# Local attention, gated layer and soft mixture of experts on one core: q and k of the last two batches read in 32-column pieces and turned by VectorE

## The chip, the cores and the metric

One Trainium2 chip, one of its cores. The metric is the device time of one execution in microseconds: 482.99 us as the median of three runs before the change (480.85 to 483.46). Times inside the execution come from one profiled execution and count from the start of its span. TensorE does the matrix products, VectorE and ScalarE elementwise work, GpSimd (POOL in the rows) elementwise work on SBUF alone, and SyncE (SP) issues the transfers between HBM and SBUF.

## The reference

```python
scores = (1 / sqrt(D)) * q @ k.T              # 4 batches, 8 heads, 576 positions, 64 columns
mask: heads 0-3 keep the last 32 positions;
      heads 4-7 keep every 4th of the last 128
attn = exp(scores - max) / (sum + 1e-9); x = attn @ v      # x: 2304 tokens x 512
h = x @ w_in; g = h - tanh(h); x = g @ w_out               # 512 -> 2048 -> 512
logits = x @ phi                                           # 32 slots
d = softmax(logits over tokens); c = softmax(logits over slots)
slot_in = d.T @ x; per expert: slot_out = relu(slot_in @ w1) @ w2
out = c @ slot_out
```

## The kernel before

Batches and chunks are numbered from 0, as in the code; the change is on batches 2 and 3, the third and the fourth.

The work is written out by hand in one order for all engines. The attention of batch 0 comes first. Then come four chunks of 512 tokens for the gated layer (the 64 tokens that each batch has left over follow later as a fifth, shorter part), and each of the first three chunks carries the attention of the next batch beside it: chunk 0 that of batch 1 (`mixed_step`, with the conversion of the weights), chunk 1 that of batch 2 and chunk 2 that of batch 3 (`phase_step`). Chunk 3 carries none. A chunk has 8 steps of two tiles of 128 hidden columns. A tile of `emit_h` is 12 products of 512 columns on TensorE (L505 to L507), followed by tanh on ScalarE (L511) and a subtraction on VectorE (L514). Its result g goes to the logits (`emit_logits`, L520, on TensorE) and is turned in 32x32 blocks on VectorE (`emit_gT`, L527).

A `phase_step` issues, in this order: the first tile; the denominators of the scores of the step before (`emit_norm`: VectorE L329 and L331, GpSimd L332); tanh and subtraction; in steps 0 and 2 a piece of the softmax over the chunk before (`sm_one`); tile turns; the second tile with its tanh and subtraction; the logits of the tiles of the step before; transposes of the probabilities (`emit_trans`, L341, copied out by ScalarE); q and k of one pair (`emit_qk`, L270); two units of scores (`emit_scores`, L308); two units of values (`emit_pv`, L362); loads; and in steps 0 to 2 another softmax piece. The pieces are `sm_a` (takes the logits out of PSUM and forms their maximum, at the chunk's end), `sm_b` and `sm_c` (the maximum over tokens, exponentials), `sm_d` (transposes, with the copy L609), `sm_e` (the sums for the slots, L643 on TensorE, L650 on VectorE) and `sm_c2` (the softmax over slots, L620 to L628).

Heads go in pairs, four pairs a batch, in the order of `PO = (2, 3, 0, 1)`: the dilated heads first. A pair has three units of scores, a batch twelve, two in each of steps 0 to 5. `load_qk` reads q and k of a pair with 96 rows on the partitions, and `emit_qk` brings the 64 columns onto the partitions: six transposes each for k and q on TensorE into PSUM, from where VectorE (k) and ScalarE (q, scaled by 1/8) copy them into a ring of two places (`qks`). For the dilated heads the copy also sorts the positions, so that those of one class lie next to each other. Scores of batches 2 and 3 are masked by an addition on VectorE (L314) and reduced to their maximum (L317); ScalarE does the exponentials (L320).

Before the change `an.qk` does pair 0 at the end of the chunk before and pairs 1 to 3 in steps 0, 2 and 3:

```python
            if an:
                an.trans(s)
                if s in (0, 2, 3):
                    an.qk(max(1, s))
                an.score(2 * s)
```

Raw q and k, v, weights, x and expert weights live in 16 equal places of SBUF (`unit`); a transfer that gets a place waits until its last reader is done. All transfers stand in SP's queue in program order. Late in the kernel the weights of the experts arrive in places that the layer's weights and tiles have left.

Of the kernel before, what the change touches and what calls it, by code (L numbers as in the profile page):

```python
# [8 lines left out]
F32 = mybir.dt.float32  # L9
# [5 lines left out]
ALU = mybir.AluOpType  # L15
# [16 lines left out]
MASKPE = 2  # L32
PO = (2, 3, 0, 1)
RAW = {
    ("out", 0): 0, ("out", 2): 1, ("out", 4): 2, ("in", 0): 3, ("in", 2): 0, ("in", 4): 1, ("out", 6): 2, ("in", 6): 3,
# [27 lines left out]
def moe_kernel(ctx: ExitStack, tc: tile.TileContext, q, k, v, w_in, w_out, phi, w1, w2, out):  # L63
    nc = tc.nc
# [4 lines left out]
    NP = H // 2  # L69
# [139 lines left out]
    def load_qk(b, p):  # L209
# [13 lines left out]
        raws[b, p] = t  # L223

    def load_v(b, p, eng):

# [59 lines left out]
    def emit_scores(b, i):  # L286
# [11 lines left out]
        for c in range(nb):  # L298
            for x in range(2):
                if nb == 4:  # L300

                    r2, qi = divmod(2 * u + c // 2, 3)
                    q0 = 288 * (c % 2) + 144 * r2
                    q0, k0 = q0 + nq * qi, q0 + max(0, nq * qi - 32)
                else:
                    q0, k0 = nq * (nb * u + c), max(0, nq * (nb * u + c) - 32)
                r = slice(64 * x, 64 * x + 64)
                nc.tensor.matmul(  # L308
                    ps[64 * x:64 * x + nr, c, :], lhsT=qT[b, p][r, q0:q0 + nr], rhs=kT[b, p][r, k0:k0 + nk],
                    start=not by_pe, stop=True, skip_group_check=True,  # L310
                )
# [213 lines left out]
    def emit_gT(ch, ft, g):  # L525

        nc.vector.transpose(out=gt[:, ft, :], in_=g)  # L527
# [230 lines left out]
    class Attn:  # L758
# [5 lines left out]
        def load(self, nqk, nv):  # L764
            while self.nqk < min(nqk, NP) or self.nv < min(nv, NP):
                if self.nqk < min(nqk, NP):
                    load_qk(self.b, PO[self.nqk])
                    self.nqk += 1
                if self.nv < min(nv, NP):
                    load_v(self.b, PO[self.nv], nc.sync)  # L770
                    self.nv += 1

        def turn(self, s):
# [5 lines left out]
            if 0 < s <= NU // 2:  # L779
                for i in (2 * s - 2, 2 * s - 1):  # L780
                    emit_trans(self.b, i)

        def qk(self, p):
            for n in range(2):
                emit_qk(self.b, PO[p], n)

# [36 lines left out]
    with tc.manual_schedule():  # L823
# [59 lines left out]

        def mixed_step(an, ch, s, xh, xl, gs):

# [48 lines left out]

        def phase_step(an, ch, s, xh, xl, gs):

# [5 lines left out]
            emit_sub(pa, gs[a])  # L942
            if s in (0, 2):
                sm_one()
# [8 lines left out]
            if an:  # L953
                an.trans(s)
                if s in (0, 2, 3):
                    an.qk(max(1, s))
                an.score(2 * s)
                an.score(2 * s + 1)
                an.values(s)
                an.load(*{0: (3, 2), 2: (4, 3), 3: (4, 4)}.get(s, (0, 0)))  # L960
            if s < 3:
                sm_one()

        an = Attn(1)
        an.nqk, an.nv = 2, 1
        for ch in range(4):
# [13 lines left out]
            for s in range(NFT // 2):  # L980
                (phase_step if ch else mixed_step)(an, ch, s, xh, xl, gs)
                if ch < 2 and s > 4:
                    if s == 5:
                        nxt = Attn(ch + 2)
                    nxt.load(*((2, 0) if s == 5 else (2, 1)))
                room[0] += sum(ROOM.get((ch, f), 0) for f in (2 * s, 2 * s + 1))
                load_experts()
            if ch:
                emit_logits(ch, NFT - 2, gs[NFT - 2])
            if nxt:  # L990
                nxt.qk(0)
            emit_logits(ch, NFT - 1, gs[NFT - 1])
            sm_queue(ch, 4)
            emit_gT(ch, NFT - 2, gs[NFT - 2])
            emit_gT(ch, NFT - 1, gs[NFT - 1])
            an = nxt
        prev = None
# [173 lines left out]
```

## Time and profile before

| | |
|---|---|
| median of three runs | 482.99 us (480.85 to 483.46) |
| the profiled execution | 480.95 us, its span 479.2 us |
| TensorE products / VectorE / ScalarE / GpSimd busy | 442.2 / 258.1 / 207.5 / 63.6 us |
| chunk 1 (157.68 to 236.97) | 79.29 us |
| chunk 2 (236.97 to 316.30) | 79.33 us |
| transposes of q and k (L270), whole kernel | 192 |

The span is the time from the first to the last instruction; the rest of the execution's time lies around it. Busy time of TensorE overlaps from one product to the next, so the length of a group is read from its start to the start of what follows.

### The profile page before, as it was taken

What the parts mean: (1) busy time and instruction counts of PE and PEld (TensorE: products, weight loads), DVE (VectorE), ACT (ScalarE), POOL (GpSimd) and SP (SyncE); (2) the same over time, 40 slices, a digit from 0 to 9 for tenths busy, and PEclk for the clock granted to TensorE, in tenths of its full rate; (3) what the DMA queues carried; (4) which work ended last, traced back from release to release, by engine and by line L of the source; (5) the groups of instructions that cost most, each with busy time, mean ns of one, the idle gap of its engine ahead of it and who ended that gap; (6) DMA issues with size and microseconds to landing.
All of it is one profiled execution on the core that took longest, in us unless ns stands there. A gap on an engine that the chain in (4) does not pass through costs nothing.

```text
span 479.2 us, 11573 instructions
## 1 busy us (share of the span) xinstructions
PE 442.2 (92%) x4711; PEld 325.9 (68%) x4711; DVE 258.1 (54%) x631; ACT 207.5 (43%) x699; POOL 63.6 (13%) x87
## 2 busy tenths in 40 slices
PE   6989888997999999999999999999999999999971
PEld 4766556776767877787786777777777879645320
DVE  1455589877976646656544775552843351232031
ACT  4877366555542373654354555422111222213131
POOL 3311313332332020111011021100000000010000
PEclk9999998998999999999999999999999999999996
DMA  9999954968252301411410310229000789999938
GB/s 247 223 248 305 255 189 133 269 219 224 91 177 60 75 0 24 102 53 51 105 29 3 87 39 1 90 77 363 1 1 0 253 320 408 348 406 409 406 152 331
DMA packets 60740, 81.15 MB, mean 169 GB/s; under 512 B 35600, under 2 KB 39440, under 8 KB 60688
## 3 DMA queue, kind: packets, MB, share of 16 engines
q1 hardware_dynamic: 60688, 80.42, 52.9%
q8 instruction: 37, 0.61, 0.6%
q14 instruction: 15, 0.12, 0.1%
HBM read 71.50 MB, written 8.91 MB: 168 GB/s over the span
## 4 chain that ended last, share of the span: by engine, by line
PE 62%; DVE 15%; ACT 9%; DMA 7%; issue 2%; POOL 2%; SPq 0%; DVEq 0%; ACTq 0%; POOLq 0%
PE h L505 12%; PE h L507 11%; PE h L506 11%; ACT mem L320 5%; DMA ex<-in_moe_w_dram 4%; PE lg L520 4%; PE mm L643 4%; PE mm L308 4%; PE h L727 3%; PE mm L362 2%; DVE cva L446 2%; PE mm L341 2%; DMA raww<-in_moe_w_out_dram 2%; PE mm L270 2%; DVE gt L527 2%
## 5 line engine op out<-in xcount | busy, mean ns | idle before, releaser
L505 PE MATMUL h<-xhi,whi 128*128 128x512 f32 x256 | 105.9, 414 | 1.1 <-DVE whi L101 0.7
L507 PE MATMUL h<-xhi,wlo 128*128 128x512 f32 x256 | 100.9, 394 | 2.0 <-POOL wlo L460 2.0
L506 PE MATMUL h<-xlo,whi 128*128 128x512 f32 x256 | 100.8, 394 | 0.0
L511 ACT ACTIVATE mem<-h 128x512 f32<-128x512 f32 x60 | 35.7, 596 | 100.3 <-PE h L507 100.1
L514 DVE TENSOR_TENSOR mem<-h,mem 128x512 f32<-128x512 f32 x60 | 41.1, 684 | 57.2 <-ACT mem L511 57.1
L505 PEld LDWEIGHTS h<-xhi,whi 128*128 128x128 f32 x256 | 48.6, 190 | 17.4 <-issue 5.3
L507 PEld LDWEIGHTS h<-xhi,wlo 128*128 128x128 f32 x256 | 48.5, 189 | 14.4 <-POOL wlo L460 3.7
L506 PEld LDWEIGHTS h<-xlo,whi 128*128 128x128 f32 x256 | 48.6, 190 | 8.9 <-DVE xlo L394 0.2
L332 POOL TENSOR_TENSOR mem<-mem 128x320 f32<-128x320 f32 (+1 forms) x48 | 33.0, 703 | 130.6 <-DVE mem L329 81.2
L394 DVE TENSOR_TENSOR xlo<-mm,xhi 128x144 fp32r<-128x144 f32 (+4 forms) x72 | 16.7, 269 | 37.0 <-ACT xhi L101 36.3
L320 ACT ACTIVATE mem<-mem 128x80 f32<-128x80 f32 (+1 forms) x84 | 29.7, 355 | 14.4 <-DVE mem L317 14.4
L308 PE MATMUL mm<-qk 64*64 64x96 f32 (+2 forms) x672 | 33.6, 243 | 2.3 <-ACT qk L278 2.1
L320 ACT ACTIVATE mem<-mm,mem 128x80 f32<-128x80 f32 (+1 forms) x84 | 26.8, 335 | 16.3 <-DVE mem L317 16.2
L527 DVE STREAM_TRANSPOSE gt<-mem 128x512 f32<-128x512 f32 x52 | 33.4, 684 | 0.0
L101 ACT COPY mem<-mm 96x384 f32<-96x384 f32 (+4 forms) x64 | 26.3, 436 | 15.8 <-PE mm L341 8.5
L308 PEld LDWEIGHTS mm<-qk 64*64 64x64 f32 (+1 forms) x672 | 26.9, 131 | 8.4 <-ACT qk L278 3.8
L341 PE MATMUL mm<-mem 112*80 112x112 f32 (+1 forms) x168 | 24.0, 272 | 6.8 <-ACT cvb L437 2.7
L460 POOL TENSOR_TENSOR wlo<-cvb,whi 128x512 fp32r<-128x512 f32 x16 | 20.6, 1287 | 73.4 <-DVE whi L101 33.7
L362 PE MATMUL mm<-mem,v 80*64 80x48 f32 (+1 forms) x672 | 26.0, 226 | 0.5 <-ACT mem L101 0.5
L362 PEld LDWEIGHTS mm<-mem,v 80*64 80x64 f32 (+1 forms) x672 | 22.1, 137 | 5.4 <-issue 2.2
L270 PE MATMUL mm<-mem,rqk 96*128 96x96 f32 x192 | 21.3, 257 | 4.2 <-DMA rqk<-in_k_dram 4.1
L341 PEld LDWEIGHTS mm<-mem 112*80 112x80 f32 (+1 forms) x168 | 16.1, 122 | 12.1 <-POOL mem L332 7.1
(169 smaller groups left out, 673.8 us busy)
## 6 DMA issues: line engine op xcount, KB each, us to landing
ex<-in_moe_w_dram SPq DMA_DIRECT2D x20, 1024.0 KB, 9.3
gt<-in_moe_w_dram SPq DMA_DIRECT2D x8, 1024.0 KB, 13.5
gt<-in_moe_w_out_dram SPq DMA_DIRECT2D x7, 1024.0 KB, 7.9
gt<-in_moe_w_in_dram SPq DMA_DIRECT2D x7, 1024.0 KB, 7.0
wo_dram<-cva SPq DMA_DIRECT2D x16, 256.0 KB, 6.5
mem<-in_moe_w_dram SPq DMA_DIRECT2D x4, 1024.0 KB, 9.9
wo<-wo_dram SPq DMA_DIRECT2D x4, 1024.0 KB, 6.8
out_dram<-o SPq DMA_DIRECT2D x8, 512.0 KB, 4.8
```

Source lines behind the costliest of these rows:

```text
L270: nc.tensor.transpose(ps[:, r, :], raw[:, 3 * th + r if p < NP // 2 else 2 * r + th], ident[0:96, 0:96])
L308: nc.tensor.matmul(ps[64 * x:64 * x + nr, c, :], lhsT=qT[b, p][r, q0:q0 + nr], rhs=kT[b, p][r, k0:k0 + nk], start=not by_pe, stop=True, sk ...
L320: nc.scalar.activation(out=pr[:, c, :], in_=ps[:, c, :], func=ACTF.Exp, bias=nm[:, c:c + 1], accum_out=sm[:, c:c + 1],)
L332: nc.gpsimd.tensor_tensor(out=pr, in0=pr, in1=rc.unsqueeze(2).to_broadcast([128, nb, nk]), op=ALU.mult)
L341: nc.tensor.transpose(ps[:, c, :], pr[0:P, c, :], ident[0:P, 0:P])
L362: nc.tensor.matmul(o[64 * hh:64 * hh + 64, col:col + nq], lhsT=vt[b, p](n, hh), rhs=pt[:, c, 64 * x:64 * x + nq], start=True, stop=True,)
L505: nc.tensor.matmul(ps, lhsT=wh, rhs=xh[:, kt, :], start=(n == 0), stop=False)
L506: nc.tensor.matmul(ps, lhsT=wh, rhs=xl[:, kt, :], start=False, stop=False)
L507: nc.tensor.matmul(ps, lhsT=wl, rhs=xh[:, kt, :], start=False, stop=(n == KT - 1))
L511: nc.scalar.activation(out=g, in_=ps, func=ACTF.Tanh)
L514: nc.vector.tensor_tensor(out=g, in0=ps, in1=g, op=ALU.subtract)
L527: nc.vector.transpose(out=gt[:, ft, :], in_=g)
```

## The change

Batches 2 and 3 (`VB`) read q and k in eight transfers a pair. The partition is a position within a block of 32 (and the half of the columns, and the head or, for the dilated heads, the parity of the position), and the pieces that follow each other on it are 32 columns, 128 bytes, of one position each. GpSimd scales the raw q by 1/8 in place, and two instructions on VectorE turn k and q in 32x32 blocks straight into the ring's place. For the dilated heads the positions of one class are then every second column, and the score products step by two on both sides. `turn_qk` comes right after the subtraction of the first tile, in steps 0, 1, 3 and 4 for pairs 0 to 3. The last logits of a chunk, `sm_a` and the last two tile turns (`last_posts`) are issued in step 0 of the next chunk behind its first tile's subtraction; the softmax pieces then come one place later.

```diff
--- before.py
+++ after.py
@@ -31,6 +31,7 @@
 CAL = 2.29
 MASKPE = 2
 PO = (2, 3, 0, 1)
+VB = (2, 3)
 RAW = {
     ("out", 0): 0, ("out", 2): 1, ("out", 4): 2, ("in", 0): 3, ("in", 2): 0, ("in", 4): 1, ("out", 6): 2, ("in", 6): 3,
     ("out", 8): 2, ("out", 10): 1, ("in", 8): 2, ("in", 10): 3, ("out", 14): 2, ("in", 14): 3,
@@ -222,6 +223,39 @@
                 nc.sync.dma_start(out=t[:, n], in_=src.rearrange("h (x a) d -> (h x) (a d)", a=12))
         raws[b, p] = t
 
+    def load_qk_blocks(b, p):
+
+        t = unit("rqk", [128, 2, S])
+        for n, src in enumerate((q, k)):
+            src = src[b, 2 * p:2 * p + 2]
+            for x in range(2):
+                if p < NP // 2:
+                    rows = src[x].rearrange("(t l) d -> l t d", l=32)
+                else:
+                    rows = src.rearrange("h (m l i) d -> i l h m d", l=32, i=2)[x]
+                for dh in range(2):
+                    dst = t[64 * x + 32 * dh:64 * x + 32 * dh + 32, n]
+                    cols = slice(32 * dh, 32 * dh + 32)
+                    if p < NP // 2:
+                        nc.sync.dma_start(out=dst.rearrange("p (t d) -> p t d", d=32), in_=rows[:, :, cols])
+                    else:
+                        nc.sync.dma_start(
+                            out=dst.rearrange("p (h m d) -> p h m d", h=2, d=32), in_=rows[:, :, :, cols]
+                        )
+        raws[b, p] = t
+
+    def turn_qk(b, p):
+
+        if not qks:
+            t = sb.tile([128, 2, 2 * S], F32, tag="qk", name="qk")
+            qks.append(Ring([t[:, 0], t[:, 1]]))
+        t = raws[b, p]
+        nc.gpsimd.tensor_scalar(out=t[:, 0], in0=t[:, 0], scalar1=0.125, scalar2=None, op0=ALU.mult)
+        qT[b, p] = qks[0].next()
+        kT[b, p] = qT[b, p][:, S:2 * S]
+        nc.vector.transpose(out=kT[b, p], in_=t[:, 1])
+        nc.vector.transpose(out=qT[b, p][:, 0:S], in_=t[:, 0])
+
     def load_v(b, p, eng):
 
         t = unit("v", [96, 24 * D])
@@ -297,16 +331,21 @@
             )
         for c in range(nb):
             for x in range(2):
+                step = 1
                 if nb == 4:
 
                     r2, qi = divmod(2 * u + c // 2, 3)
                     q0 = 288 * (c % 2) + 144 * r2
                     q0, k0 = q0 + nq * qi, q0 + max(0, nq * qi - 32)
+                    if b in VB:
+                        q0, k0 = (288 * (c % 2) + r2 + 2 * (t - 288 * (c % 2) - 144 * r2) for t in (q0, k0))
+                        step = 2
                 else:
                     q0, k0 = nq * (nb * u + c), max(0, nq * (nb * u + c) - 32)
                 r = slice(64 * x, 64 * x + 64)
                 nc.tensor.matmul(
-                    ps[64 * x:64 * x + nr, c, :], lhsT=qT[b, p][r, q0:q0 + nr], rhs=kT[b, p][r, k0:k0 + nk],
+                    ps[64 * x:64 * x + nr, c, :], lhsT=qT[b, p][r, q0:q0 + step * (nr - 1) + 1:step],
+                    rhs=kT[b, p][r, k0:k0 + step * (nk - 1) + 1:step],
                     start=not by_pe, stop=True, skip_group_check=True,
                 )
         pr = prs.next()[:, 0:nb * nk].rearrange("p (c k) -> p c k", c=nb)
@@ -764,7 +803,7 @@
         def load(self, nqk, nv):
             while self.nqk < min(nqk, NP) or self.nv < min(nv, NP):
                 if self.nqk < min(nqk, NP):
-                    load_qk(self.b, PO[self.nqk])
+                    (load_qk_blocks if self.b in VB else load_qk)(self.b, PO[self.nqk])
                     self.nqk += 1
                 if self.nv < min(nv, NP):
                     load_v(self.b, PO[self.nv], nc.sync)
@@ -779,10 +818,6 @@
             if 0 < s <= NU // 2:
                 for i in (2 * s - 2, 2 * s - 1):
                     emit_trans(self.b, i)
-
-        def qk(self, p):
-            for n in range(2):
-                emit_qk(self.b, PO[p], n)
 
         def trans(self, s):
             if 0 < s <= NU // 2:
@@ -881,7 +916,7 @@
             nc.vector.tensor_tensor(out=part[:, :, 1, :], in0=c, in1=part[:, :, 0, :].bitcast(F32), op=ALU.subtract)
             cst[b] = part
 
-        def mixed_step(an, ch, s, xh, xl, gs):
+        def mixed_step(an, ch, s, xh, xl, gs, posts):
 
             a, b = 2 * s, 2 * s + 1
             if s == 0:
@@ -932,7 +967,7 @@
                 emit_logits(ch, a - 1, gs[a - 1])
             emit_logits(ch, a, gs[a])
 
-        def phase_step(an, ch, s, xh, xl, gs):
+        def phase_step(an, ch, s, xh, xl, gs, posts):
 
             a, b = 2 * s, 2 * s + 1
             pa, gs[a] = emit_h(xh, xl, a), gring.next()
@@ -940,7 +975,11 @@
                 an.norms(s - 1)
             emit_tanh(pa, gs[a])
             emit_sub(pa, gs[a])
-            if s in (0, 2):
+            if an and s in QKS:
+                turn_qk(an.b, PO[QKS.index(s)])
+            if s == 0:
+                posts()
+            elif s < 3:
                 sm_one()
             for n in range(0 if s == 2 else max(0, a - 2), 0 if s == 1 else a):
                 emit_gT(ch, n, gs[n])
@@ -952,8 +991,6 @@
                 emit_logits(ch, a - 1, gs[a - 1])
             if an:
                 an.trans(s)
-                if s in (0, 2, 3):
-                    an.qk(max(1, s))
                 an.score(2 * s)
                 an.score(2 * s + 1)
                 an.values(s)
@@ -961,8 +998,9 @@
             if s < 3:
                 sm_one()
 
+        QKS = (0, 1, 3, 4)
         an = Attn(1)
-        an.nqk, an.nv = 2, 1
+        an.nqk, an.nv, posts = 2, 1, None
         for ch in range(4):
             xh, xl = xhi[ch], xlo[ch]
             if ch == 3:
@@ -978,7 +1016,7 @@
                 gring = gts
             gs, nxt = {}, None
             for s in range(NFT // 2):
-                (phase_step if ch else mixed_step)(an, ch, s, xh, xl, gs)
+                (phase_step if ch else mixed_step)(an, ch, s, xh, xl, gs, posts)
                 if ch < 2 and s > 4:
                     if s == 5:
                         nxt = Attn(ch + 2)
@@ -987,13 +1025,16 @@
                 load_experts()
             if ch:
                 emit_logits(ch, NFT - 2, gs[NFT - 2])
-            if nxt:
-                nxt.qk(0)
-            emit_logits(ch, NFT - 1, gs[NFT - 1])
-            sm_queue(ch, 4)
-            emit_gT(ch, NFT - 2, gs[NFT - 2])
-            emit_gT(ch, NFT - 1, gs[NFT - 1])
-            an = nxt
+
+            def last_posts(ch=ch, gs=gs):
+                emit_logits(ch, NFT - 1, gs[NFT - 1])
+                sm_queue(ch, 4)
+                emit_gT(ch, NFT - 2, gs[NFT - 2])
+                emit_gT(ch, NFT - 1, gs[NFT - 1])
+
+            if ch == 3:
+                last_posts()
+            an, posts = nxt, last_posts
         prev = None
         for s in range(NFT // 2):
             a = 2 * s
```

VectorE where chunk 1 begins; before, with the two copies of k (`COPY qk`) of pair 0 and of pair 1:

```order
L514 TENSOR_TENSOR mem<-h,mem 128x512
L101 COPY qk<-mm 128x3x2x48 x2
L552 COPY mem<-lg 128x128
L554 TENSOR_REDUCE mem<-mem 128x1
L527 STREAM_TRANSPOSE gt<-mem 128x512 x2
L514 TENSOR_TENSOR mem<-h,mem 128x512
L562 TENSOR_REDUCE mem<-mm 1x32
```

and VectorE at the same place now, where the first row holds the last subtraction of chunk 0 and the first of chunk 1:

```order
L553 TENSOR_TENSOR mem<-h,mem 128x512 x2
L256 STREAM_TRANSPOSE qk<-rqk 128x576
L257 STREAM_TRANSPOSE qk<-rqk 128x576
L591 COPY mem<-lg 128x128
L593 TENSOR_REDUCE mem<-mem 128x1
L566 STREAM_TRANSPOSE gt<-mem 128x512 x2
L553 TENSOR_TENSOR mem<-h,mem 128x512
L353 TENSOR_TENSOR mem<-mm,mem 128x320
```

The turns of pair 0 stand between the first tile's subtraction and `sm_a`; the masks (L353, before L314) follow the second tile's subtraction with no copies between.

VectorE in step 3 of chunk 1, from the denominators on; before:

```order
L329 TENSOR_SCALAR mem<-mem 128x4
L331 RECIPROCAL mem<-mem 128x4
L514 TENSOR_TENSOR mem<-h,mem 128x512
L527 STREAM_TRANSPOSE gt<-mem 128x512 x2
L514 TENSOR_TENSOR mem<-h,mem 128x512
L101 COPY qk<-mm 128x3x96 x2
L314 TENSOR_TENSOR mem<-mm,mem 128x288
```

and VectorE in step 3 now:

```order
L368 TENSOR_SCALAR mem<-mem 128x4
L370 RECIPROCAL mem<-mem 128x4
L553 TENSOR_TENSOR mem<-h,mem 128x512
L256 STREAM_TRANSPOSE qk<-rqk 128x576
L257 STREAM_TRANSPOSE qk<-rqk 128x576
L566 STREAM_TRANSPOSE gt<-mem 128x512 x2
L553 TENSOR_TENSOR mem<-h,mem 128x512
L353 TENSOR_TENSOR mem<-mm,mem 128x288
```

The two turns have moved ahead of the tile turns and of the second subtraction, where the two copies stood behind them.

GpSimd in chunk 1 now, where before the row of the scaling (L253) was not there:

```order
L253 TENSOR_SCALAR rqk<-rqk 128x576
L371 TENSOR_TENSOR mem<-mem 128x320 x2
L253 TENSOR_SCALAR rqk<-rqk 128x576
L633 COPY mem<-mem 128x512
L371 TENSOR_TENSOR mem<-mem 128x320 x4
L253 TENSOR_SCALAR rqk<-rqk 128x576
L371 TENSOR_TENSOR mem<-mem 128x288 x2
```

Each scaling but the first stands behind the two multiplies of its step.

## Rows read from the trace of the kernel before

**Rows 1.** Windows of chunks 1 and 2: length, busy us and instructions by engine, clock, DMA.
```profile
157.68:236.97 79.29, 78.21 (x892) 61.34 (x889) 46.19 (x120) 40.63 (x152) 8.68 (x13) 1.00 0.21 49
236.97:316.30 79.33, 77.23 (x880) 60.29 (x876) 46.36 (x120) 40.22 (x150) 8.68 (x13) 1.00 0.19 45
```

**Rows 2.** TensorE in order of time where chunk 2 begins, and where chunk 3 begins.
```profile
235.47 1.21 PE L270 MATMUL mm<-mem,rqk 96*128 96x96 f32 x12
236.62 0.43 PE L520 MATMUL lg<-mem 128*32 128x128 f32 x8
236.97 0.50 PE L505 MATMUL h<-xhi,whi 128*128 128x512 f32 x1
...
239.86 0.48 PE L505 MATMUL h<-xhi,whi 128*128 128x512 f32 x1
...
315.94 0.43 PE L520 MATMUL lg<-mem 128*32 128x128 f32 x8 [0.62 <-DVE mem L514]
```

**Rows 3.** TensorE in order of time, end of step 0 of chunk 1.
```profile
163.40 1.16 PE L270 MATMUL mm<-mem,rqk 96*128 96x96 f32 x12
164.48 1.32 PE L308 MATMUL mm<-qk 64*64 64x80 f32 x32
165.74 0.24 PE L569 MATMUL mm<-mem 1*32 1x1 f32 x8
```

**Rows 4.** Groups by line and shape, whole kernel: count, busy us, mean ns, idle before.
```profile
L514 DVE TENSOR_TENSOR mem<-h,mem 128x512 f32<-128x512 f32 x60 | 41.1, 684 | 57.2 <-ACT mem L511 57.1
L511 ACT ACTIVATE mem<-h 128x512 f32<-128x512 f32 x60 | 35.7, 596 | 100.3 <-PE h L507 100.1
L527 DVE STREAM_TRANSPOSE gt<-mem 128x512 f32<-128x512 f32 x52 | 33.4, 684 | 0.0
L460 POOL TENSOR_TENSOR wlo<-cvb,whi 128x512 fp32r<-128x512 f32 x16 | 20.6, 1287 | 73.4 <-DVE whi L101 33.7 <-DVE mem L329 30.2 <-issue 4.8
L332 POOL TENSOR_TENSOR mem<-mem 128x320 f32<-128x320 f32 x24 | 16.9, 720 | 67.5 <-DVE mem L329 48.6 <-DVE mem L331 10.1 <-ACT cva L437 6.5
L101 DVE COPY qk<-mm 128x288 f32<-128x288 f32 x20 | 10.9, 599 | 0.4 <-PE mm L270 0.4
```

**Rows 5.** VectorE, ScalarE and TensorE in order of time, steps 0 to 2 of chunk 1.
```profile
165.66 0.47 DVE L314 TENSOR_TENSOR mem<-mm,mem 128x320 f32<-128x320 f32 x1
...
178.16 0.58 ACT L609 COPY mem<-mm 128x512 f32<-128x512 f32 x1
...
178.83 4.47 PE L643 MATMUL mm<-gt,mem 32*32 32x512 f32 x128
```

**Rows 6.** TensorE in step 2 of chunk 1, VectorE in step 2 of chunk 2.
```profile
187.54 1.35 PE L270 MATMUL mm<-mem,rqk 96*128 96x96 f32 x12
...
268.29 1.18 DVE L101 COPY qk<-mm 128x288 f32<-128x288 f32 x2
```

**Rows 7.** GpSimd and TensorE in order of time, step 3 of chunk 1.
```profile
197.47 1.40 POOL L332 TENSOR_TENSOR mem<-mem 128x320 f32<-128x320 f32 x2 [16.91 <-DVE mem L329]
...
198.24 1.26 PE L341 MATMUL mm<-mem 112*80 112x112 f32 x8 [0.74 <-POOL mem L332]
199.34 1.16 PE L270 MATMUL mm<-mem,rqk 96*128 96x96 f32 x12
200.43 1.31 PE L308 MATMUL mm<-qk 64*64 64x96 f32 x24
```

**Rows 8.** Groups by line and shape: weight loads of transposes, without and with a step of two.
```profile
L538 PEld LDWEIGHTS mm<-mem 128*128 128x128 f32 x32 | 3.4, 140 | 1.6 <-issue 1.2 <-DVE tb L650 0.2 <-ACT g L540 0.2
...
L742 PEld LDWEIGHTS mm<-mem 128*128 128x128 f32 x16 | 2.5, 205 | 2.9 <-issue 2.9
```

**Rows 9.** SP's issue of k, all landings of L217, and the window of these loads.
```profile
188.93 1.25 SPq L217 DMA_DIRECT2D rqk<-in_k_dram  x2
...
DMA to landing us min/median/max: 2.7/4.8/9.1
...
188.90:199.00 10.10, 9.26 (x109) 7.33 (x110) 6.22 (x21) 5.84 (x26) 1.40 (x2) 1.00 0.50 105
```

## The prediction

> **What bounds the kernel now.** I read the busy time by stage first, then TensorE's order of time through chunks 1 and 2, then what VectorE, ScalarE and GpSimd do beside it. The windows of the two chunks [rows 1] are what the change works on: TensorE is busy 78.21 of 79.29 us in chunk 1 and 77.23 of 79.33 in chunk 2 at full granted clock, VectorE 46 and ScalarE 40 of the same time. So an instruction taken off TensorE is worth its length there, as long as nothing else becomes late. What follows (chunk 3, the remainder, the experts) starts from TensorE's progress: expert places and the weight slots become free as TensorE finishes with them, so I let a gain made before 316 us pass through to the end in full.
>
> The order of time at a chunk's end [rows 2] shows the transposes standing as a filler: twelve of them between the logits of tile 14 and those of tile 15, from 235.47 to 236.62. At the end of chunk 2, where there is no next batch, the same place shows 0.62 us of waiting for VectorE's subtraction. In step 0 [rows 3] they take 163.40 to 164.48. Nothing waits for q and k data in these chunks.
>
> **The change part by part.**
>
> 1. *Chunk ends, before chunks 1 and 2.* Twelve transposes go. The logits of tile 15 move behind the next chunk's first tile, so the subtraction they need is long done there and no new gap opens. 236.62 less 235.47 is 1.15 us each [rows 2], two chunks: -2.3.
>
> 2. *Step 0.* 164.48 less 163.40 is 1.08 each, two chunks: -2.2. The cover: scores 0 and 1 now need VectorE's two turns. After the first tile VectorE waits for tanh (0.60 by the row), subtracts (0.68), and turns k and q. A turn of 128x512 takes 0.684, so 576 columns are estimated at 0.684 x 576/512 = 0.77; the four in a row are 0.60+0.68+1.54 = 2.8 us [rows 4], and with hand-overs some 2.9. TensorE meanwhile does the moved logits (0.35, 236.97 less 236.62) and the second tile (a tile takes 2.89, 236.97 to 239.86), 3.2 us [rows 2]. It fits with 0.3 us to spare. GpSimd's scaling is done early here, since the data landed a chunk step before.
>
> 3. *Step 1* gives something back. VectorE's turns of pair 1 stand ahead of the softmax piece that moved here from step 0 (the running maximum and, on ScalarE, its exponential), and ScalarE's tanh of the second tile and its copies of the transposed probabilities stand behind that. GpSimd must multiply two units (0.72 each) before it scales q; the scaling of 576 columns lies between 0.72 (the multiply of 320) and 1.287 x 576/512 = 1.45 (the two-input subtraction of 512) [rows 4]; I take 1.0, as it has one input. Following this chain: the masks of step 0 start at about 164.1 instead of 165.66, so everything on ScalarE and VectorE behind them can be 1.5 early, while TensorE is 2.2 early; the copy that the slot sums of step 2 wait for, which ended at 178.74 just ahead of them at 178.83 [rows 5], comes some 1.3 early. Of 2.2 gained at that point 1.3 is left: +0.9 in chunk 1, and +1.1 in chunk 2, where the moved piece has one more exponential. Both: +2.0 (between +1.0 and +3.0).
>
> 4. *Step 2.* The transposes that start at 187.54 go (1.35 with the last one's tail), -1.3. In chunk 2 VectorE is the late one (four rescalings and four turns ahead); there its two copies (1.18) go, and I count -1.2 [rows 6]. Together -2.5.
>
> 5. *Step 3.* TensorE waits for GpSimd before the probabilities already (0.74), because VectorE came late to the denominators [rows 7]. Now VectorE has subtraction, k turn, the wait for GpSimd's scaling (which starts when the multiplies end, 198.87), and q turn ahead of score 6: 198.87 + 1.0 + 0.77 = 200.6, on the old clock. TensorE, without its transposes from 199.34, would be ready at 199.4. So the 1.09 that goes is replaced by a wait of 1.2: +0.1 each, and +0.1 to +0.3 in chunk 2: +0.4 together (-0.5 to +1.2 with the two ends of GpSimd's price). What is late next is VectorE's subtraction of the second tile, behind two turns and two tile turns; it has until the second tile of step 4.
>
> 6. *Step 4.* The turn is needed for score 9 alone, behind two tiles, logits, probabilities and score 8; 0. ScalarE loses two copies of q a pair; it hid them. VectorE's balance is two turns (1.54) for two copies (2 x 0.599): +0.3 a pair on an engine that is busy under 60%.
>
> 7. *End of chunk 2.* The wait of 0.62 for the subtraction goes [rows 2]: -0.6.
>
> 8. *Scores of the dilated heads* now read every second column for both operands: six steps with 32 passes each (two units, four blocks, two halves, two passes a float32 product), in pairs that run side by side, so 96 pairs of passes. Now 32 passes take 165.74 less 164.48, 1.26 us: 79 ns a pair [rows 3]. The only row with such a step is the weight load of the experts' transposes: 205 ns where the same shape without a step takes 140 [rows 8], 65 more for 128 columns, or 33 for 64. Low end 0, if weight loads stay hidden behind the other half's pass and moving columns cost nothing; a quarter of 33 ns exposed gives 96 x 8 = +0.8; high end 79 more a pair, both sides at half pace, 96 x 79 = +7.6. I take +0.8, because the loads overlap the passes of the other half. [...]
>
> 9. *Loads.* Eight transfers of 72 KB instead of two or four; SP issues one in 0.63 (1.25 for two), so 5.0 us a pair instead of 2.5, landing 4.8 after issue [rows 9]. In 188.90 to 199.00 the queue moved pair 3's q and k and 8 blocks of v, 2304 + 1728 pieces of 256 bytes, at 0.50 of 16 engines: 81 us for 4032, 20 ns each. 4608 pieces at that price are 5.8 us a pair over 16 engines. Pair 3 is the tight one: loaded at the end of step 2 and now turned in step 4, over 13 us later; 5.0 + 4.8 fits. Price 0. SP moves nothing else past them that is urgent.
>
> Sum: -2.3 - 2.2 + 2.0 - 2.5 + 0.4 - 0.6 + 0.8 = -4.4. The profiled execution took 480.95, so 476.6; the median of the runs is 482.99, 2.0 above it, which gives 478.6. I forecast 478.0, nearer to the median.
>
> **Rivals.**
> - *The turns keep what the transposes gave up.* If VectorE reaches the q turn 0.5 us later than counted (GpSimd at 1.45, or the turn longer than the tile turns say), step 0 loses its 0.3 of spare and more, steps 1 and 3 another half each: some 2 to 3 us, leaving -2 to -1: 480.5 to 482. For it: GpSimd's form isn't in the trace. Against: the tile turn is, 52 times, without spread. 0.20.
> - *Columns at half pace.* TensorE reads both operands with a step; if that doubles a pair (79 ns more), term 8 is +7.6 instead of +0.8 and the sum +2.4: 485.4 from the median, slower. It turns to a loss at 5.2/96 = 54 ns a pair. For it: the load of 205 against 140. Against: that row's excess is at most 33 ns a load here, with two halves overlapping. 0.10.
> - *Late data.* Pieces of 128 bytes at 60 ns instead of 20 would need 4608 x 60/16 = 17 us; pair 3 would be some 4 us late in both chunks, with v behind it: +8, net +4, 487. Against: 256-byte pieces take 20 ns here. [...] The trace already runs 256-byte pieces, and double their price, 11.5 us a pair, still lands in time. 0.04.
> - *Everything is kept*: steps 1 and 3 give nothing back (GpSimd at 0.72, the slot sums not held): -7 to -8, 471 to 475 from either base. 0.08.
> - That the order isn't as the change says I exclude: the built program has the turns and the logits where the text puts them.
>
> **How the numbers follow.** The forecast has 0.58, with -2.5 to -6.5 around it: 475 to 480.5. About 0.5% (2.4 us) is what a measurement of this kernel can tell. Faster: the forecast's cases and "everything kept", less a little of the edge, 0.65. Same: the rival of the turns, 0.21. Slower: half pace and late data, 0.14. The range takes in the forecast, most of the turns' rival and the bases' 2 us: 473.5 to 483.5; left out are the slow rivals' core and the best end.
>
> **What would show it.** Right: no transposes of q and k in chunks 1 and 2, scores of step 0 following the second tile without idle time, a TensorE wait of about 1 us ahead of score 6 ended by VectorE's q turn, the slot sums of step 2 starting about 1.3 + 1.1 early, chunk 1 some 2.3 and chunk 2 some 2.1 shorter, a pair of passes at 79 to 95 ns. Wrong: pairs over 130 ns, VectorE waiting for data at a turn, or an idle TensorE in step 0.

## The result, and the profile after

The changed kernel takes 485.38 us (median of 17 runs, 484.08 to 488.48), the kernel before on the same chip 481.94: a ratio of 1.0063, 95% interval 1.0044 to 1.0082. It is slower by 3.4 us, where 4.4 less was forecast, and above the range. Its profiled span is 483.4 us.

The windows of chunks 1 and 2, each from its first tile to the next chunk's, answer to [rows 1] (length, busy us and instructions of TensorE, its weight loads, VectorE, ScalarE and GpSimd, granted clock, DMA):

```profile
156.14:237.68 81.54, 77.57 (x844) 59.62 (x840) 47.01 (x120) 36.24 (x143) 15.19 (x17) 0.96 0.27 51
237.68:319.92 82.24, 77.65 (x844) 59.57 (x840) 48.55 (x122) 35.29 (x142) 13.57 (x16) 0.96 0.21 46
```

The transposes are gone (48 and 36 instructions less on TensorE), yet both chunks are longer, by 2.25 and 2.91 us, and the granted clock is no longer 1.00. GpSimd's busy time is up by 6.5 in chunk 1. TensorE in order of time through step 3 of chunk 1, beside [rows 7], shows where. Line numbers have moved with the edit: L380 transposes the probabilities, L346 is the scores, L401 the values, L544 to L546 the products of a tile; in brackets stands how long the engine was idle before, and what ended that:

```profile
196.46 1.26 PE L380 MATMUL mm<-mem 112*80 112x112 f32 x8 [0.69 <-POOL mem L371]
199.66 1.21 PE L346 MATMUL mm<-qk 64*64 64x96 f32 x24 [1.94 <-DVE qk L257]
200.80 1.95 PE L401 MATMUL mm<-mem,v 80*64 80x48 f32 x32
202.68 0.80 PE L544 MATMUL h<-xhi,whi 128*128 128x512 f32 x1
203.27 0.63 PE L545 MATMUL h<-xlo,whi 128*128 128x512 f32 x1
...
208.05 0.39 PE L545 MATMUL h<-xlo,whi 128*128 128x512 f32 x1
```

TensorE waits 1.94 us ahead of score 6 for the q turn. Then the values take 1.95 instead of 1.14, and a product of 512 columns 0.63 instead of 0.39, until 208. The windows of 1 us over this place name the reason in the column after GpSimd's, the granted clock:

```profile
198.00:199.00 1.00, 0.00 (x0) 0.00 (x0) 0.26 (x1) 0.28 (x1) 0.70 (x1) 1.00 0.00 0
199.00:200.00 1.00, 0.34 (x8) 0.37 (x10) 1.00 (x2) 0.00 (x0) 0.00 (x0) 1.00 0.00 0
200.00:201.00 1.00, 1.00 (x26) 0.88 (x23) 1.00 (x3) 0.00 (x0) 0.00 (x0) 0.91 0.26 62
201.00:202.00 1.00, 1.00 (x22) 1.00 (x22) 0.97 (x3) 0.00 (x0) 0.00 (x0) 0.50 0.89 201
...
207.00:208.00 1.00, 1.00 (x4) 0.77 (x4) 0.00 (x0) 0.00 (x0) 1.00 (x2) 0.68 0.00 0
208.00:209.00 1.00, 1.00 (x6) 0.81 (x6) 0.35 (x1) 0.60 (x1) 0.70 (x1) 1.00 0.00 0
```

Behind the two waits of 0.69 and 1.94 us, with 1.26 us of work between them, TensorE's granted clock goes from 1.00 to 0.50 for some 7 us. Chunk 2 shows the same, from the window of 282 to that of 289. GpSimd and VectorE in order of time tell what the q turn waited for:

```profile
195.69 1.40 POOL L371 TENSOR_TENSOR mem<-mem 128x320 f32<-128x320 f32 x2 [15.64 <-DVE mem L368]
197.05 1.65 POOL L253 TENSOR_SCALAR rqk<-rqk 128x576 f32<-128x576 f32 x1
...
196.28 0.77 DVE L256 STREAM_TRANSPOSE qk<-rqk 128x576 f32<-128x576 f32 x1
198.74 0.78 DVE L257 STREAM_TRANSPOSE qk<-rqk 128x576 f32<-128x576 f32 x1 [1.69 <-POOL rqk L253]
```

The turns take what was estimated (0.77). GpSimd's scaling takes 1.65 and stands behind the two multiplies. TensorE's largest waits from 150 to 330 us, in total (us, times, longest):

```profile
PE mm L346 <- DVE qk L257: 3.9, 2, 1.9
PE mm L401 <- ACT mem L102: 1.8, 4, 0.8
PE mm L380 <- POOL mem L371: 1.8, 2, 1.1
PE mm L682 <- ACT mem L648: 0.9, 2, 0.5
```

The time of chunk 1 by steps, from the start of each step's first tile to the next one's (us). "Forecast" is the kernel before with the prediction's terms (the 0.4 of term 8 spread over steps 0 to 2, the 0.35 of the moved logits counted in step 0 and out of the rest); the last two columns are experiments below.

| | before | forecast | changed | factor in the mask | early turn |
|---|---|---|---|---|---|
| step 0 | 8.22 | 7.6 | 7.59 | 7.62 | 7.58 |
| steps 1 and 2 | 25.25 | 25.1 | 25.73 | 24.52 | 24.53 |
| step 3 | 11.59 | 11.7 | 13.22 | 10.68 | 9.34 |
| step 4 | 9.03 | 9.0 | 11.30 | 9.03 | 9.06 |
| rest | 25.20 | 23.7 | 23.70 | 23.69 | 23.69 |
| chunk 1 | 79.29 | 77.2 | 81.54 | 75.54 | 74.20 |

So the gain came where it was expected, at step 0 and at the end. It was lost in steps 1 to 4.

### The profile page after: what moved, and what is told of

Same layout as the page of the kernel before. It is cut to its first block, busy times and chain, and to the rows that moved or that the text cites. A ratio compares the mean times of both kernels' runs of the same rounds, so it can differ in the third digit from the quotient of the medians.

```text
span 483.4 us, 11432 instructions
## 1 busy us (share of the span) xinstructions
PE 440.9 (91%) x4615; PEld 322.5 (67%) x4615; DVE 260.4 (54%) x631; ACT 198.6 (41%) x683; POOL 76.6 (16%) x95
## 4 chain that ended last, share of the span: by engine, by line
PE 52%; DVE 17%; ACT 12%; DMA 8%; issue 4%; POOL 3%; SPq 2%; DVEq 0%; ACTq 0%; POOLq 0%
PE h L544 10%; PE h L546 9%; PE h L545 9%; ACT mem L359 7%; DMA ex<-in_moe_w_dram 4%; PE mm L682 4%; PE lg L559 3%; PE h L766 3%; PE mm L346 3%; PE mm L401 2%; DVE cva L485 2%; DMA raww<-in_moe_w_out_dram 2%; DVE mem L356 2%; DVE mem L553 2%; DMA rqk<-in_k_dram 2%
## 5 line engine op out<-in xcount | busy, mean ns | idle before, releaser
L544 PE MATMUL h<-xhi,whi 128*128 128x512 f32 x256 | 108.5, 424 | 1.1 <-DVE whi L102 0.7
L546 PE MATMUL h<-xhi,wlo 128*128 128x512 f32 x256 | 102.7, 401 | 2.0 <-POOL wlo L499 2.0
L545 PE MATMUL h<-xlo,whi 128*128 128x512 f32 x256 | 102.6, 401 | 0.0
L544 PEld LDWEIGHTS h<-xhi,whi 128*128 128x128 f32 x256 | 49.8, 195 | 18.0 <-issue 5.9
L546 PEld LDWEIGHTS h<-xhi,wlo 128*128 128x128 f32 x256 | 49.5, 193 | 14.8 <-POOL wlo L499 3.7
L545 PEld LDWEIGHTS h<-xlo,whi 128*128 128x128 f32 x256 | 50.0, 195 | 9.2 <-DVE xlo L433 0.2
L346 PE MATMUL mm<-qk 64*64 64x96 f32 (+2 forms) x672 | 34.1, 244 | 5.8 <-DVE qk L257 3.9
L346 PEld LDWEIGHTS mm<-qk 64*64 64x64 f32 (+1 forms) x672 | 27.4, 131 | 12.5 <-issue 6.1
L499 POOL TENSOR_TENSOR wlo<-cvb,whi 128x512 fp32r<-128x512 f32 x16 | 20.6, 1288 | 73.4 <-DVE mem L368 30.2
L380 PE MATMUL mm<-mem 112*80 112x112 f32 (+1 forms) x168 | 23.9, 271 | 7.1 <-ACT cvb L476 2.7
L401 PE MATMUL mm<-mem,v 80*64 80x48 f32 (+1 forms) x672 | 27.6, 234 | 1.8 <-ACT mem L102 1.8
L401 PEld LDWEIGHTS mm<-mem,v 80*64 80x64 f32 (+1 forms) x672 | 23.6, 146 | 7.0 <-ACT mem L102 2.6
L380 PEld LDWEIGHTS mm<-mem 112*80 112x80 f32 (+1 forms) x168 | 16.1, 122 | 12.3 <-POOL mem L371 7.3
L559 PE MATMUL lg<-mem 128*32 128x128 f32 x480 | 22.3, 282 | 0.3 <-DVE mem L553 0.3
```

The costliest lines, as they stand in the source:

```text
L346: nc.tensor.matmul(ps[64 * x:64 * x + nr, c, :], lhsT=qT[b, p][r, q0:q0 + step * (nr - 1) + 1:step], rhs=kT[b, p][r, k0:k0 + step * (nk - ...
L380: nc.tensor.transpose(ps[:, c, :], pr[0:P, c, :], ident[0:P, 0:P])
L401: nc.tensor.matmul(o[64 * hh:64 * hh + 64, col:col + nq], lhsT=vt[b, p](n, hh), rhs=pt[:, c, 64 * x:64 * x + nq], start=True, stop=True,)
L544: nc.tensor.matmul(ps, lhsT=wh, rhs=xh[:, kt, :], start=(n == 0), stop=False)
L545: nc.tensor.matmul(ps, lhsT=wh, rhs=xl[:, kt, :], start=False, stop=False)
L546: nc.tensor.matmul(ps, lhsT=wl, rhs=xh[:, kt, :], start=False, stop=(n == KT - 1))
```

## The experiments

Theory A: GpSimd's scaling makes TensorE wait in step 3, and the clock that falls behind the wait costs more than the wait itself. The rivals: the loads of small pieces, the strided scores or VectorE's turns. I compare the lengths of chunks 1 and 2 beside the total, since chunk 0, which is the same in all kernels, varies from one execution to the next (last section).

**The wait filled.** TensorE gets products nobody reads where it waits:

```
+    def fill(n):
+        ps = mm([128, 512])
+        w = ident.bitcast(BF16)
+        for _ in range(n):
+            nc.tensor.matmul(ps[:, 0:256], lhsT=w[:, 0:128], rhs=w, start=True, stop=True)
...
                 an.trans(s)
+                if s == 3:
+                    fill(18)
                 an.score(2 * s)
```

> The changed kernel with 18 products of 256 columns, whose results nobody reads, put on TensorE in step 3 between the probabilities and score 6, where it now waits 1.94 us for VectorE's q turn; what the kernel computes is unchanged. Theory A (GpSimd's scaling, 1.65 us long and queued behind two multiplies, makes that wait, and the granted clock that falls to 0.50 behind it costs about 3.3 us more in each of chunks 1 and 2): the products fill the wait, the clock stays at 1.00 in step 4, the half-clock time (2 x 3.3) comes back: 478 to 480 us, 5 to 7 below the changed kernel. Rival B (the loads of 128-byte pieces that run in the same stretch, or the strided scores, slow TensorE there): the fall stays, and the time is that of the changed kernel, 485 to 488.

Measured: 481.06 us beside 482.88 of the kernel before, ratio 0.9968 (0.994 to 0.9996); the chunks take 78.77 and 79.46 us. TensorE in order of time:

```profile
199.56 1.26 PE L386 MATMUL mm<-mem 112*80 112x112 f32 x8 [0.70 <-POOL mem L377]
200.66 2.13 PE L211 MATMUL mm<-mem 128*128 128x256 bf16 x18
202.76 1.21 PE L352 MATMUL mm<-qk 64*64 64x96 f32 x24
203.90 1.14 PE L407 MATMUL mm<-mem,v 80*64 80x48 f32 x32
```

Score 6 starts 1.94 us after the probabilities end, as in the changed kernel, but the values take 1.14 instead of 1.95, and the clock stays at 1.00 in both chunks. Loads and strides are untouched. The clock by itself is worth 81.54 - 78.77 = 2.77 and 82.24 - 79.46 = 2.78, 5.5 together; I had put it at 3.3 each, so the total is 1 us above the expectation.

**The scaling ahead of the multiplies.** `scale_q` holds GpSimd's scaling, taken out of `turn_qk`:

```
+            if an and s in QKS:
+                scale_q(an.b, PO[QKS.index(s)])
             if an:
                 an.norms(s - 1)
```

> The changed kernel with GpSimd's scaling of q issued ahead of the two multiplies of the same step instead of behind them; the work is the same. Theory A: the scaling is done before VectorE comes to the turns, the wait ahead of score 6 is under 0.5 us, the clock stays at 1.00, both parts come back: 2 x (1.5 + 3.3) less some 1 us for multiplies that come later, 475 to 478 us. Rival B (loads or strides): no more than the wait itself comes back, 482 to 483, with the clock still falling in step 4.

Measured: 475.71 beside 482.88, ratio 0.9851 (0.9799 to 0.9904); chunks 75.55 and 79.30. The same instructions in another order on GpSimd take some 10 us off the changed kernel (by its ratio an estimated 1.0063 x 482.88 = 485.9 here). Chunk 2 is the odd one; TensorE there:

```profile
273.32 1.26 PE L383 MATMUL mm<-mem 112*80 112x112 f32 x8 [1.09 <-POOL mem L374]
274.71 2.05 PE L349 MATMUL mm<-qk 64*64 64x96 f32 x24
```

The wait ahead of the scores is gone, but in this execution the clock fell behind the one of 1.09 ahead of the probabilities: the scores run at half pace (2.05 us instead of 1.21), and the clock reads 0.50 from 275 to 281, where products of 512 columns take 0.63 instead of 0.39. The profiled execution is the slowest of the four (473.10 to 478.11). That fall costs about 79.30 - 76.16 = 3.1 by the next kernel.

**The factor in the mask addition**, with GpSimd's scaling left out:

```
-            nc.vector.tensor_tensor(out=pr, in0=ps, in1=mask, op=ALU.add)
+            nc.vector.scalar_tensor_tensor(out=pr, in0=ps, scalar=0.125, in1=mask, op0=ALU.mult, op1=ALU.add)
```

> The changed kernel without GpSimd's scaling: the factor 0.125 is applied where VectorE adds the mask to the scores, in the same instruction. Theory A: as with the scaling moved ahead, 474 to 478 us, the wait ahead of score 6 ends with the second turn alone and is under 0.5 us, and the wait ahead of the probabilities is that of the kernel before or less. Rival C (VectorE's two turns themselves hold score 6): a wait of over 1 us stays with VectorE's turn behind it, the clock still falls, 482 to 485.

Measured: 475.73 beside 482.88, ratio 0.9847 (0.9792 to 0.9902). Windows of the two chunks:

```profile
158.22:233.76 75.54, 74.31 (x844) 57.05 (x840) 46.67 (x120) 36.24 (x143) 8.74 (x13) 1.00 0.29 55
233.76:309.92 76.16, 74.34 (x844) 57.05 (x840) 48.21 (x122) 35.19 (x142) 8.74 (x13) 1.00 0.22 49
```

The clock is 1.00 throughout, and VectorE's turns hold score 6 by 0.1 us only, so the rival of the turns falls. The addition of the mask takes no longer with the factor in it (480 ns for 320 columns, 479 in the changed kernel). In step 3 of chunk 2 the wait ahead of the probabilities is there as in the kernel above:

```profile
273.60 1.26 PE L379 MATMUL mm<-mem 112*80 112x112 f32 x8 [1.10 <-POOL mem L370]
274.99 1.21 PE L345 MATMUL mm<-qk 64*64 64x96 f32 x24
```

1.10 here with no fall, 1.09 there with one: a wait of this size can be followed by a fall and need not be.

**The wait put into the kernel before.**

```
+            if an and s == 3:
+                t = qT[an.b, PO[2]][:, 0:S]
+                for _ in range(2):
+                    nc.gpsimd.tensor_scalar(out=t, in0=t, scalar1=1.0, scalar2=None, op0=ALU.mult)
```

> The kernel before, with nothing of the change, and two multiplications by 1.0 on GpSimd over the q of step 3 (128x576 each, in place) ahead of score 6, so that TensorE waits there as it does in the changed kernel or longer; the result is the same. Theory A (a wait at this place is enough for the clock to fall): the granted clock falls to 0.50 in step 4 of chunks 1 and 2, the time is 2 x (about 1.8 + 3.3), some 10 us above the kernel before, 490 to 495. Rival B (the fall needs the change's loads or strides): the clock stays at 1.00 and only the wait is added, 485 to 487.

Measured: 486.51 beside 482.88, ratio 1.0082 (1.0049 to 1.0114); chunks 81.02 and 81.08. TensorE in step 3 of chunk 1:

```profile
198.99 1.26 PE L341 MATMUL mm<-mem 112*80 112x112 f32 x8 [0.79 <-POOL mem L332]
200.09 1.16 PE L270 MATMUL mm<-mem,rqk 96*128 96x96 f32 x12
203.02 1.21 PE L308 MATMUL mm<-qk 64*64 64x96 f32 x24 [1.78 <-POOL qk L946]
```

Theory A fails as I put it. The waits are there, 0.79 and 1.78, the clock stays at 1.00, and the chunks grow by the wait alone (1.73 and 1.75). Either the fall does need the change's loads or strides, or it matters that the transposes stand between the two waits here.

**Both waits close together, in the kernel before.** The fourth pair's transposes go to step 4, and GpSimd's extra work is shorter:

```
+            if an and s == 3:
+                t = qT[an.b, PO[2]][:, 0:S]
+                for t in (t, t[:, 0:288]):
+                    nc.gpsimd.tensor_scalar(out=t, in0=t, scalar1=1.0, scalar2=None, op0=ALU.mult)
...
-                if s in (0, 2, 3):
-                    an.qk(max(1, s))
+                if s in (0, 2, 4):
+                    an.qk((1, 0, 2, 0, 3)[s])
```

> The kernel before with the q and k transposes of the fourth pair moved from step 3 to step 4, and one and a half multiplications by 1.0 on GpSimd over the q of step 3 (128x576 and 128x288), so that TensorE waits, works 1.26 us and waits again as in the changed kernel, with no loads of 128-byte pieces, no strided scores and no VectorE turn; the result is the same. The kernel with the wait alone (two multiplications) kept its clock with the transposes between its two waits. Theory A (two waits of about 0.7 and 1.9 us with only the probabilities between them are enough): the granted clock falls to 0.50 in step 4 of both chunks, and the time is 2 x (1.9 + 3.3), 10 us above the kernel before, 491 to 494. Rival B (the fall needs something else of the change): the clock stays at 1.00 and only the wait is added, some 4 us, 485 to 488.

Measured: 494.69 beside 481.53, ratio 1.0272 (1.0236 to 1.0308); chunks 84.73 and 84.88. TensorE in order of time, then two windows of 1 us:

```profile
200.47 1.26 PE L341 MATMUL mm<-mem 112*80 112x112 f32 x8 [0.74 <-POOL mem L332]
203.77 2.19 PE L308 MATMUL mm<-qk 64*64 64x96 f32 x24 [2.05 <-POOL qk L946]
```

```profile
202.00:203.00 1.00, 0.00 (x0) 0.00 (x0) 0.15 (x1) 0.29 (x1) 0.92 (x2) 1.00 0.00 0
...
204.00:205.00 1.00, 1.00 (x16) 1.00 (x16) 0.00 (x0) 0.00 (x0) 0.00 (x0) 0.50 0.00 0
```

The clock falls in both chunks (its mean is 0.96 in each), in chunk 1 with no transfer under way (the DMA share is 0.00 in these windows), and in both with none of the change's loads, no strided column and no VectorE turn of q or k. So the fall needs nothing of the loads, the strides or the turns; it comes behind two waits with only 1.26 us of work between them. The second wait is also 0.27 longer than in the experiment before, so the work between the waits and their length are not told apart. The total is a little over the expected range; the wait is 2.05 instead of 1.9, and the moved transposes' copies add 0.39 of waiting in step 4 of each chunk.

**The logits alone**, in the kernel before (transposes stay; `last_posts` as in the change):

```
+            elif s < 3:
+                sm_one()
...
-            emit_logits(ch, NFT - 1, gs[NFT - 1])
+            an, posts = nxt, last_posts
```

> The kernel before with only the last logits of a chunk moved behind the next chunk's first tile (and the softmax pieces with them, as in the change); all transposes stay on TensorE. Terms 1 and 7 of the prediction: what the move brings by itself is the wait of 0.62 us at the end of chunk 2, so 0 to 1 us less than before, 481.5 to 483. Rival: the softmax pieces that come a half step later hold step 1 or 2, 1 to 3 us more than before.

Measured: 482.81 beside 481.53, ratio 1.0014 (0.9979 to 1.0049): no difference that can be told. The chunks take 79.41 and 78.89: only in chunk 2 is something gained, 0.44, about the wait of 0.62.

**Large pieces**, in the kernel with the factor in the mask (the text below counts batches from 1, its 3 and 4 are `VB`):

```
-            for x in range(2):
...
+            nc.sync.dma_start(out=t[:, n], in_=src.rearrange("h (x a) d -> (h x) (a d)", a=9))
```

> The kernel with the factor in the mask addition, with q and k of batches 3 and 4 loaded by one transfer each in pieces of 2304 bytes instead of four in pieces of 128, into the same tiles. It leaves out the placement that the turns need, so that its scores are of other rows. Term 9 of the prediction (the loads cost nothing): the time is that of the kernel with the factor in the mask addition, 475 to 477. Rival (the small pieces hold other transfers up): 2 us or more less, 472 to 474.

Measured: 475.17 beside 481.53, ratio 0.9884 (0.984 to 0.9927); chunks 75.52 and 76.15, within 0.02 of the small pieces (75.54, 76.16). The small pieces cost nothing here.

**The early turn.** With the factor in the mask, step 3's waits of 0.77 and 1.10 remain ahead of the probabilities, because VectorE is late. The third pair's turns go where VectorE waits for ScalarE in step 2 (2.22 us in chunk 1 of the changed kernel), and the norms ahead of the softmax piece:

```
-            if an:
+            if an and s != 3:
                 an.norms(s - 1)
...
-            if an and s in QKS:
+            if an and s in QKS and s != 3:
                 turn_qk(an.b, PO[QKS.index(s)])
...
                 an.score(2 * s + 1)
+                if s == 2:
+                    turn_qk(an.b, PO[2])
                 an.values(s)
+                if s == 2:
+                    an.norms(2)
```

> The kernel with the factor in the mask addition, and in chunks 1 and 2 the third pair's two turns put into step 2 behind its scores, where VectorE waits for ScalarE, and the norms of step 2 ahead of the softmax piece there. Theory A: TensorE's waits ahead of the probabilities of step 3 (0.77 and 1.10) and ahead of its scores (0.1 each) go, and with them what is left of the danger to the clock: 472 to 475, 1 to 3 below the kernel with the factor in the mask addition. Rival: the turns hold the subtractions of the values or the norms on VectorE, and the copies behind them on ScalarE, and the time is the same or 1 us more.

Measured: 471.52 beside 481.53, ratio 0.9786 (0.9761 to 0.9812), the fastest of all, 10 us below the kernel before; chunks 74.20 and 74.52. All of TensorE's waits from 150 to 335 us:

```profile
PE h L545 <- POOL wlo L498: 0.6, 1, 0.6
PE mm L400 <- ACT mem L102: 0.5, 2, 0.2
PE mm L681 <- ACT mem L647: 0.3, 1, 0.3
```

**Neighbouring columns**, in the kernel with the early turn:

```
-                    if b in VB:
-                        q0, k0 = (288 * (c % 2) + r2 + 2 * (t - 288 * (c % 2) - 144 * r2) for t in (q0, k0))
-                        step = 2
```

> The kernel with the early turn, with the scores of the dilated heads reading neighbouring columns instead of every second one. It leaves out the choice of columns, so that those scores are of other rows; the shapes and counts are the same. Term 8 of the prediction (a step of two costs 0 to 8 ns a pair of passes, 0.8 us in all): 471 to 472, the same as the kernel with the early turn within the measurement. Rival (half pace, 79 ns a pair): 7 us less, 463 to 466.

Measured: 471.72 beside 481.65, ratio 0.9779 (0.9728 to 0.983); chunks 74.18 and 74.48. The dilated scores of both chunks as a group, with a step of two and without:

```profile
L345 PE MATMUL mm<-qk 64*64 64x80 f32 x192 | 8.2, 233 | 0.0
```

```profile
L342 PE MATMUL mm<-qk 64*64 64x80 f32 x192 | 7.9, 233 | 0.0
```

0.3 us of busy time in all, 0.06 of the chunks' length.

**The early turn, with GpSimd's scaling kept** (the changed kernel with the two moves of the early turn and nothing else):

> The changed kernel with GpSimd's scaling kept, and only the third pair's scaling and turns moved into step 2 behind its scores, with the norms of step 2 ahead of the softmax piece there. Theory A (the scaling costs by its place behind the multiplies of step 3, not by itself): both waits of step 3 and the fall of the clock go, step 1 still gives back its 1.5 to 1.8 a chunk: 473 to 476. Rival (a scaling of 1.65 us holds the q turn and what is behind it on VectorE wherever it stands): waits of 1 us or more at step 2's or step 3's probabilities, 478 or more.

Measured: 476.98 beside 481.65, ratio 0.9883 (0.9837 to 0.9929); chunks 75.64 and 76.32, the clock 1.00 in both. Three of TensorE's waits from 150 to 335 us:

```profile
PE mm L401 <- ACT mem L102: 1.8, 4, 0.8
PE mm L682 <- ACT mem L648: 0.9, 2, 0.5
PE mm L346 <- DVE qk L257: 0.4, 1, 0.4
```

The waits of step 3 are gone; those of step 1 (values, slot sums) are as in the changed kernel. Behind the multiplies of step 1 the scaling of 1.65 us still costs 1.4 to 1.8 a chunk against the early turn without it. It need not: ahead of the multiplies in every step it left chunk 1 as long as without it (75.55 and 75.54). The early turn with the scaling ahead wasn't run. The total is 1 us over the upper end expected, the ratio's interval reaches into it.

## Why the prediction was wrong

In the windows of [rows 1] the prediction's terms give -2.1 in chunk 1 and -1.1 in chunk 2, and -1.15 at the end of chunk 0, which lies in neither; its last paragraph puts -2.3 and -2.1 on the two chunks instead. In the profiled executions chunk 1 begins 1.54 earlier, the chunks are 2.25 and 2.91 longer, and what follows takes 0.6 more, 4.2 in all. By its terms:

- Terms 1 (*chunk ends*, -1.15 each) and 7 (*end of chunk 2*, -0.6): right. The rest of chunk 1 is 1.50 shorter, the 1.15 and the 0.35 of the moved logits.
- Term 2 (*step 0*, -1.08 each, nothing new): right. It is 0.63 shorter with 0.35 of logits moved in; nothing waits for the turns.
- Terms 3 (*step 1* gives back 0.9 and 1.1) and 4 (*step 2*, -1.3 and -1.2): mechanism right, sizes a little off. Steps 1 and 2 together should have come out 0.4 and 0.1 shorter; they are 0.48 and 0.28 longer. What GpSimd's scaling gives back is 1.2 in each chunk (25.73 against 24.52 without it in chunk 1). Even without it the two steps are only 0.7 and 0.9 shorter than before; what took the rest wasn't separated.
- Term 5 (*step 3*): this term failed. The prediction took GpSimd's scaling at 1.0 us, between 0.72 and 1.45, "as it has one input". The lower end was a multiply of 320 columns, not brought to 576; per column it would have been 1.30. The scaling takes 1.65, above the upper end, and the wait ahead of score 6 is 1.94 instead of 1.2. That is 0.7 of the miss in chunk 1.
- Term 6 (*step 4*) at 0: failed with it, and this is the larger part. No term, rival or bound held the clock. Its fall costs 2.77 and 2.78 by the filled wait (in chunk 1, 0.8 of it still in step 3), 5.5 of the 8.4 us between the terms and the measured lengths of the two chunks.
- Term 8 (*strided scores*) at +0.8: 0.3 at most, 8.2 us of busy time with the step against 7.9 without it. The longer weight load of [rows 8] did not show: in steps 0 to 2 of chunk 1 a weight load of the scores has a median of 133 ns before and after, a pass 229 before and 230 after.
- Term 9 (*loads*) at 0: right.

The rival "the turns keep what the transposes gave up" named the right mechanism, GpSimd at its upper end and losses in steps 1 and 3, at 2 to 3 us. The two slower rivals did not occur. Slower came about by a way that wasn't listed: none of the prediction's signs of being wrong came (VectorE waited at a turn, but for GpSimd and not for data), and the wait ahead of score 6, ended by VectorE's q turn, was one of its signs of being right.

It could have been seen. The transposes that the change removes would have been the work between the two waits. And in the trace before, outside the two chunks that I read, chunk 0 shows the clock fall behind a wait of 2.69 us:

```profile
73.64 1.48 PE L341 MATMUL mm<-mem 112*80 112x112 f32 x8 [2.69 <-ACT cvb L437]
```

```profile
75.00:76.00 1.00, 1.00 (x7) 1.00 (x6) 1.00 (x3) 0.53 (x1) 0.00 (x0) 0.50 0.14 39
```

A wait that a change is forecast to add or lengthen on TensorE needs a second price from such a place, and a chance, as the fall need not come (last section): there the clock was at or near 0.50 for some 3.5 us.

## What to carry to other kernels

Taking work off the bounding engine pays only if what replaces it is ready in time at each place; here the same turns gave +3.4 us as the change has them, some -7 with GpSimd's scaling ahead of its multiplies or folded into the mask addition, and -10 with the third pair's turns moved as well. Put such work into a slot in which its engine already waits, ahead of what must wait for others, and fold a scaling into an operation that passes over the data anyway (here the mask addition took 480 ns with the factor and 479 without it). When work between two waits on TensorE is removed, read the granted clock behind waits of that size elsewhere in the trace and give the fall a term.

## What was not expected of the hardware

- A multiplication by a constant on GpSimd, one input, in place, cost more per column than one with two inputs: the groups by line of the changed kernel give 1651 ns for 576 columns (2.9 ns each), and 1288 for 512 (2.5) and 720 for 320 (2.3) with two. The number of inputs alone tells little: a copy of 512 columns, each value read four times, takes 610 (1.2).

```profile
L499 POOL TENSOR_TENSOR wlo<-cvb,whi 128x512 fp32r<-128x512 f32 x16 | 20.6, 1288 | 73.4 <-DVE mem L368 30.2 <-DVE whi L102 30.1 <-DVE cvb L102 4.8
L371 POOL TENSOR_TENSOR mem<-mem 128x320 f32<-128x320 f32 x24 | 17.0, 720 | 95.0 <-DVE mem L368 43.3 <-DVE mem L370 41.5 <-ACT cva L476 6.6
...
L253 POOL TENSOR_SCALAR rqk<-rqk 128x576 f32<-128x576 f32 x8 | 13.2, 1651 | 0.0
L633 POOL COPY mem<-mem 128x512 f32<-128x512 f32 x4 | 2.4, 610 | 73.9 <-ACT mem L619 73.9
```

- The clock fell behind waits of 0.69 and 1.94 us with 1.26 of work between, and stayed at 1.00 behind 0.79 and 1.78 with the transposes between. Behind a single wait it fell in the trace of one kernel (1.09) and not in that of another (1.10), with the same products around it. What else decides there stays open.
- In chunk 0, where the instructions are the same in all kernels, the wait of 2.69 us stands in the traces of the kernel before and of the changed kernel, and the clock fell around it in both, from 74 to 78 us. With neighbouring columns it fell there from 75 to 79, in the early turn with the scaling kept from 73 to 80. With the factor in the mask it did not fall, behind the same wait:

```profile
74.53 1.26 PE L379 MATMUL mm<-mem 112*80 112x112 f32 x8 [2.69 <-ACT cvb L475]
```

```profile
75.00:76.00 1.00, 0.90 (x10) 0.79 (x9) 1.00 (x3) 0.85 (x3) 0.15 (x1) 1.00 0.93 356
```

So a part of the spread between runs of one kernel can come from such falls; that wasn't tested by itself.
